# A two-layer sliding-window attention and token-mixing kernel: score bursts of four row tiles, PV in 64x32 tiles with a ones column, normalisation through DRAM, and the first token-mixing matmul in parts inside attention

## The chip, the cores and the metric

The kernel runs on one core of a Trainium2 chip. The metric is the device time of one execution in microseconds (us), quoted as the median of several executions. The engines are called PE (TensorE matmuls), PEld (TensorE weight loads, which overlap PE), DVE (VectorE), ACT (ScalarE), POOL (GpSimd) and SP (SyncE, which issues the DMAs here). An execution counts as slow when it is over 1.5% above the fastest one of the same kernel.

## The reference, cut to what matters

The input is 2048 tokens of 512 features. Two blocks alternate, two layers of each: windowed attention with 32 heads of 16 features (window 256), and an MLP that mixes tokens, with a hidden size of 1792.

```python
def _A_ref(x, wqkv, wo):                       # attention
    H = 32; Dh = 16; W = 256
    q, k, v = ...                              # x @ wqkv, split by heads
    scores = einsum("bhqd,bhkd->bhqk", q, k) * (Dh ** -0.5)
    mask = (i - j >= 0) & (i - j < W)
    p = softmax(where(mask, scores, -1e9))
    return einsum("bhqk,bhkd->bhqd", p, v) ... @ wo

def _B_ref(x, w1, b1, w2, b2):                 # MLP over the tokens
    h = _layernorm(x)
    u = gelu(einsum("bsd,sf->bdf", h, w1) + b1)    # sums over ALL 2048 tokens
    y = einsum("bdf,fs->bds", u, w2) + b2
    return y.transpose(0, 2, 1)

x = x + A(layernorm(x)); x = x + B(layernorm(x))   # twice
```

Attention only looks 256 tokens back, so it runs in four chunks of 512 tokens. And `u` sums over all tokens: each token tile's term of u needs the finished attention, the output projection `wo` and two LayerNorms of that tile, but different tiles' terms can be added up at different times.

## The kernel before

Both kernels record their operations as a graph. A greedy list scheduler inside the kernel then fixes, at build time and with estimated costs, the order of every engine and the place of every buffer. On the chip each engine goes through its list strictly in order.

One group of eight heads (`o`, four groups; a row tile `r` of 32 rows holds two heads) of one chunk (`m`) of attention before, shortened, with plain words for some calls:

```python
for k in ...:                                   # five pieces of 512 score columns (four in chunk 0)
    for u0 in range(0, len(lanes), 2):          # two row tiles per burst
        ts = Tile(psum2)                        # two PSUM banks
        def f_sc(...):
            for j, q0, n, c0 in runs:
                for i, r in enumerate(rr):      # rr = two row tiles of 32 rows
                    e.matmul(PS[:, 2*ts.slot+i, c0*64:(c0+n)*64],
                             lhsT=kbd[32*r:32*r+32, ...], rhs=qT[32*r:32*r+32, ...],
                             tile_position=(32*r, 0), ...)
        op("scalar", exp of both banks -> pt)   # 128 x 1024
    op("vector", f_mask, ...)                   # masks multiplied into pt
# values and denominators: two passes over pt, in 128x32 tiles
for dst, den in ((tO, False), (tDen, True)):
    for r in range(4):
        w = onesbd[:] if den else vbd[:, tkk.slot, jj, 4*o+r, :]
        e.matmul(PS[32*r:32*r+32, 4+dst.slot, ...], lhsT=w, rhs=pt[...], tile_position=(0, 32*r), ...)
# normalisation on the core itself
rl = Ln(tDen); rl = Exp(-rl)                    # ACT, 512 columns each
oT = tO * rl                                    # DVE, straight from PSUM
# ... cut ...
def u_phase(w1t):                               # all of u after attention
    for fb ...: for tt ...: for s0 in range(0, NT, 4):
        matmuls(PS[u], lhsT=w1b[...], rhs=xh_sb[:, sc, :])     # 16 token tiles summed in PSUM
    op("scalar", gelu: PSUM -> uT)
```

The softmax here doesn't subtract the row's maximum and nothing guards it: scores larger than these inputs give would overflow.

Of the kernel before, what the change touches and what calls it, by code (L numbers as in the profile page):

```python
# [2 lines left out]

# [3 lines left out]
dt = mybir.dt  # L7
# [3 lines left out]
P = 128  # L11
INF = float("inf")


class Pool:


    def __init__(self, name, n):
        self.name = name
        self.free = {i: [] for i in range(n)}  # L20
        self.classes = {}
# [14 lines left out]
class Op:  # L36
    __slots__ = ("idx", "eng", "fn", "cost", "lat", "prio", "deps", "users", "ndeps", "tiles", "start", "end",
                 "done", "seq", "dma", "extra", "order")


class Graph:


    ENGS = ("tensor", "vector", "scalar", "gpsimd", "sync")
    NDMA = 24
# [9 lines left out]
    def op(self, eng, fn, reads=(), writes=(), cost=100.0, lat=60.0, prio=None, dma=False, after=(), holds=()):  # L55
        o = Op()
        o.idx, o.eng, o.fn, o.cost, o.lat, o.dma = len(self.ops), eng, fn, cost, lat, dma
        o.prio = prio
        o.users, o.extra, o.order = [], [], []
        deps = {}  # L60
        tiles = {}
# [32 lines left out]
    def _alloc_time(self, o):  # L94

        t, want = 0.0, {}
        for tl in o.tiles:
            if tl.slots is None:
                pool = tl.pool
                n = want[id(pool)] = want.get(id(pool), 0) + tl.n  # L100
                q = pool.classes.get(tl.cls)
                if (q and q[0] + n > q[1]) or len(pool.free) < n:
                    return INF
                ts = sorted(max([x.done for x in ops], default=0.0) for ops in pool.free.values())
                t = max(t, ts[n - 1])
        return t

    def _alloc(self, o):
        for tl in o.tiles:
            if tl.slots is None:  # L110
                pool = tl.pool
                order = sorted(pool.free, key=lambda s: (max([x.done for x in pool.free[s]], default=0.0), s))[:tl.n]
                tl.slots = sorted(order)
                for s in tl.slots:
                    last = {}
                    for x in pool.free.pop(s):
                        if x.dma:
                            last[("d", x.idx)] = x
                        elif x.eng not in last or last[x.eng].seq < x.seq:
                            last[x.eng] = x  # L120
                    o.extra.extend(last.values())
                if tl.cls in pool.classes:
                    pool.classes[tl.cls][0] += tl.n
            tl.ops.append(o)
# [9 lines left out]

    def schedule(self):
# [4 lines left out]
        dma_free = 0.0  # L140
        for o in self.ops:
            if o.ndeps == 0:
                ready[o.idx] = 0.0
                cand[o.eng].append(o)
        left = len(self.ops)
        while left:
            best = None
            for e in self.ENGS:
                m = INF
                ests = []  # L150
                for o in cand[e]:
                    t = max(ready[o.idx], free[e])
                    if any(tl.slots is None for tl in o.tiles):
                        t = max(t, self._alloc_time(o))
                    ests.append(t)
                    if t < m:
                        m = t
                if m < INF and (best is None or m < best[0]):
                    pick = None
                    for o, t in zip(cand[e], ests):  # L160
                        if t <= m:
                            pr = (o.prio if o.prio is not None else ready[o.idx], o.idx)
                            if pick is None or pr < pick[0]:
                                pick = (pr, o)
                    best = (m, e, pick[1])
            if best is None:
                raise RuntimeError("scheduler stuck: " + str({e: len(c) for e, c in cand.items()}))
            m, e, o = best
            cand[e].remove(o)
            self._alloc(o)  # L170
            o.start = m
            if o.dma:
                free[e] = m + 600.0
                dma_free = max(dma_free, m + 600.0) + o.cost
                o.end = dma_free
                o.done = dma_free + 1500.0
            else:
                o.end = free[e] = m + o.cost
                o.done = o.end + o.lat
            o.seq = len(self.order[e])  # L180
            self.order[e].append(o)
            self._release(o)
            for u in o.users:
                u.ndeps -= 1
                ready[u.idx] = max(ready.get(u.idx, 0.0), o.done)
                if u.ndeps == 0:
                    cand[u.eng].append(u)
# [3 lines left out]
    def emit(self, block):  # L191

# [5 lines left out]
        allops = sorted(self.ops, key=lambda o: (o.start, o.idx))  # L198
# [13 lines left out]

# [5 lines left out]
        while pending:  # L218
            moved = False
            for e in self.ENGS:  # L220
                while ptr[e] < len(self.order[e]):
                    o = self.order[e][ptr[e]]
                    need = [d for d in {x.idx: x for x in o.deps + o.extra}.values()
                            if not (e == "tensor" and d.eng == "tensor")]
# [41 lines left out]
def mm_cost(n, cols):  # L266
    return n * (cols / 2.4 + 4.0)
# [10 lines left out]
def pool_cost(n, ptrs=0):  # L278
    return 195 + n / 1.4 + 83 * ptrs


def stepped(v, n, step):

    p, l, c = [list(a) for a in v.ap]
    return bass.AP(v.tensor, v.offset, [p, l, [step, n], c])


def attention_plan(first):

# [18 lines left out]
def bass_interleave_layers__sliding_block__mixer_token_mlp__prompt_kernel(  # L308
# [15 lines left out]
    NC = 4  # L324
# [465 lines left out]
```

## Time and profile before

| | before |
|---|---|
| median time | 593.61 us (4 executions, 592.83 to 595.7) |
| profiled execution | span 589.2 us, mean granted TensorE clock 0.967 |
| attention of layer 1 / layer 2 (first to last exponential) | 172.3 / 194.2 us |
| from the last exponential to the last gelu (the tails) | 63.1 / 67.7 us |

These are lines of the profile's page: busy time of each engine with its share of the span, the chain of work that ended last, and groups of instructions (line, engine, operation, tiles, shapes, count, then busy us and mean ns of one, then idle time before them and what ended most of it).

```profile
PE 533.3 (91%) x6171; PEld 240.1 (41%) x6240; DVE 299.5 (51%) x610; ACT 339.1 (58%) x400; POOL 152.8 (26%) x266
...
PE 57%; ACT 20%; DVE 14%; POOL 4%; DMA 3%; issue 2%; DVEq 0%; POOLq 0%
...
L600 ACT ACTIVATE pt<-PS 128x1024 bf16<-128x1024 f32 (+1 forms) x304 | 288.8, 1033 | 88.1 <-PE PS L587 71.4
L587 PE MATMUL PS<-qT,kbd 32*128 32x320 bf16 (+4 forms) x1440 | 120.9, 262 | 12.0 <-ACT pt L600 9.4
...
L648 PE MATMUL PS<-pt,vbd 128*32 128x320 bf16 (+4 forms) x1440 | 86.4, 270 | 7.7 <-DVE pt L621 2.8
...
L648 PE MATMUL PS<-pt,onesbd 128*32 128x320 bf16 (+4 forms) x1440 | 82.7, 267 | 0.0
```

PE is busy 91% of the span and holds 57% of the chain: as a whole the kernel is bound by PE. 2880 matmuls do values and denominators, half of them only for the denominators.

The next view cuts the span into stages. Each line has the stretch and its length, then the busy time (and count) of PE, PEld, DVE, ACT and POOL, then the granted clock, the DMA share and GB/s. The stretches are attention of layer 1, its tail with u, y and QKV of layer 2, attention of layer 2, its tail, and y with the output.

```profile
17.90:190.20 172.30, 155.77 (x2570) 73.17 (x2588) 118.00 (x245) 155.60 (x182) 68.80 (x109) 0.96 0.10 25
190.20:253.30 63.10, 59.91 (x290) 25.71 (x294) 7.73 (x18) 12.08 (x17) 3.04 (x8) 0.98 0.37 101
253.30:278.80 25.50, 24.07 (x166) 11.93 (x170) 18.03 (x37) 1.33 (x2) 10.31 (x22) 1.00 0.55 150
278.80:473.00 194.20, 180.11 (x2624) 80.19 (x2657) 125.57 (x245) 156.71 (x182) 61.45 (x99) 0.96 0.09 26
473.00:540.70 67.70, 65.24 (x313) 28.07 (x318) 7.73 (x18) 12.12 (x17) 3.04 (x8) 0.98 0.29 78
540.70:589.20 48.50, 39.80 (x173) 17.45 (x176) 11.18 (x16) 0.01 (x1) 0.00 (x0) 0.96 0.53 157
```

Average shares hide the stages: in attention ACT and PE are both busy about 90% of layer 1, while in the first tail PE is busy 60 of 63 us and ACT only 12.

Last, a piece of PE's timeline (start, length, line, tiles, shapes, count). One line can hold several matmuls of a burst; the drawn lengths overlap because ends are modelled, so the burst's pitch is read from the starts.

```profile
71.58 0.39 PE L587 MATMUL PS<-qT,kbd 32*128 32x192 bf16 x4
71.90 1.06 PE L499 MATMUL PS<-xhT,wqkv 128*128 128x512 bf16 x4
72.89 0.39 PE L587 MATMUL PS<-qT,kbd 32*128 32x320 bf16 x4
73.22 0.60 PE L499 MATMUL PS<-xhT,wqkv 128*128 128x512 bf16 x2
...
74.07 0.21 PE L648 MATMUL PS<-pt,vbd 128*32 128x64 bf16 x4
...
74.63 0.31 PE L587 MATMUL PS<-qT,kbd 32*128 32x320 bf16 x2
```

From 71.90 to 72.89 four dense matmuls of 512 columns pass, 0.216 us each plus one gap of about 0.11 us. A score burst takes 0.33 us to the next matmul (72.89 to 73.22), plus the gap ahead of it: 0.43 us for only 0.21 us of streaming. That is the waste that the change goes after. The Trainium skill, "TensorEngine Tiling (Array Packing)", section Key Properties, says that changing the tiling mode drains TensorE; the gaps on both sides of the burst shown here fit it.

### The profile page before, as it was taken

The numbers are of one execution on the slowest core, as the hardware profiler recorded it, in microseconds if no ns is written. First come the engines' busy times: TensorE is split into PE (matmuls) and PEld (weight loads), VectorE is DVE, ScalarE is ACT, GpSimd is POOL, SyncE is SP. The second block draws the span as 40 slices with busy tenths as digits, with TensorE's granted clock in tenths as the row PEclk, the third lists the DMA queues.
The fourth block names the chain that finished last, engine by engine and source line by source line (L and its number), as shares of the span: only waits on it lengthen the run. The fifth ranks groups of instructions, "written<-read, shape, count | busy, mean of one in ns | idle before, by whom it ended". The sixth has DMA issues, their size and how long they took to land.

```text
span 589.2 us, 13839 instructions
## 1 busy us (share of the span) xinstructions
PE 533.3 (91%) x6171; PEld 240.1 (41%) x6240; DVE 299.5 (51%) x610; ACT 339.1 (58%) x400; POOL 152.8 (26%) x266
## 2 busy tenths in 40 slices
PE   4879999999988989989999999999998799997897
PEld 1435444444333434444344434434433343443343
DVE  5986665865873400056766466856687341001021
ACT  0678999699898121110998992299869821111000
POOL 3772433444320200015315212621453001000000
PEclk9989999999995999999999999999999589999899
DMA  8920000000000055572020022202000005251663
GB/s 276 225 54 3 3 1 2 3 2 2 1 2 2 1 143 142 143 197 63 2 63 3 2 59 69 63 3 61 5 2 3 1 1 142 71 143 28 186 187 117
DMA packets 68299, 36.55 MB, mean 62 GB/s; under 512 B 4752, under 2 KB 68240, under 8 KB 68240
## 3 DMA queue, kind: packets, MB, share of 16 engines
q1 hardware_dynamic: 68240, 35.66, 21.8%
q8 instruction: 49, 0.80, 0.6%
q14 instruction: 10, 0.08, 0.0%
HBM read 33.56 MB, written 2.10 MB: 61 GB/s over the span
## 4 chain that ended last, share of the span: by engine, by line
PE 57%; ACT 20%; DVE 14%; POOL 4%; DMA 3%; issue 2%; DVEq 0%; POOLq 0%
ACT pt L600 17%; PE PS L722 15%; PE PS L708 15%; PE PS L587 8%; PE PS L499 7%; PE PS L648 6%; DVE stats L438 4%; PE PS L524 4%; DVE x_sb L677 2%; POOL rstd L449 2%; PE PS L674 2%; DVE pt L621 2%; DVE xh_sb L451 2%; ACT rl L661 1%; ACT rl L663 1%
## 5 line engine op out<-in xcount | busy, mean ns | idle before, releaser
L600 ACT ACTIVATE pt<-PS 128x1024 bf16<-128x1024 f32 (+1 forms) x304 | 288.8, 1033 | 88.1 <-PE PS L587 71.4
L587 PE MATMUL PS<-qT,kbd 32*128 32x320 bf16 (+4 forms) x1440 | 120.9, 262 | 12.0 <-ACT pt L600 9.4
L722 PE MATMUL PS<-uT,w2b 128*128 128x512 bf16 x429 | 105.9, 385 | 10.8 <-DMA w2b<-in_B_w_dram 4.8
L708 PE MATMUL PS<-xh_sb,w1b 128*128 128x512 bf16 x436 | 101.0, 383 | 3.0 <-DVE xh_sb L451 1.0
L726 DVE SCALAR_TENSOR_TENSOR x_sb<-PS,b2col,x_sb 128x512 bf16<-128x512 f32 x32 | 22.9, 746 | 141.8 <-PE PS L722 141.8
L648 PE MATMUL PS<-pt,vbd 128*32 128x320 bf16 (+4 forms) x1440 | 86.4, 270 | 7.7 <-DVE pt L621 2.8
L621 DVE TENSOR_TENSOR pt<-pt,ldm 128x1024 bf16<-128x1024 bf16 (+2 forms) x104 | 65.8, 632 | 52.0 <-ACT pt L600 51.7
L648 PE MATMUL PS<-pt,onesbd 128*32 128x320 bf16 (+4 forms) x1440 | 82.7, 267 | 0.0
L587 PEld LDWEIGHTS PS<-qT,kbd 32*128 32x128 bf16 x1440 | 40.5, 94 | 99.6 <-ACT pt L600 58.1
L715 ACT ACTIVATE uT<-PS,b1col 128x512 bf16<-128x512 f32 x28 | 19.2, 687 | 98.2 <-PE PS L708 98.2
L499 PE MATMUL PS<-xhT,wqkv 128*128 128x512 bf16 x227 | 68.5, 393 | 6.1 <-issue 4.4
L447 POOL TENSOR_SCALAR rstd<-agg 128x1 f32<-128x1 f32 x64 | 16.1, 251 | 220.1 <-DVE agg L440 217.6
L708 PEld LDWEIGHTS PS<-xh_sb,w1b 128*128 128x128 bf16 x448 | 43.3, 98 | 56.8 <-issue 3.2
L510 POOL TENSOR_SCALAR kbd<-stg,par 128x512 bf16<-128x512 bf16 x64 | 50.1, 795 | 62.2 <-DVE stg L507 62.0
L722 PEld LDWEIGHTS PS<-uT,w2b 128*128 128x128 bf16 x448 | 39.4, 98 | 63.2 <-issue 9.4
L536 POOL TENSOR_SCALAR vbd<-stg,half 128x512 bf16<-128x512 bf16 x64 | 49.5, 784 | 48.8 <-DVE stg L533 45.4
L648 PEld LDWEIGHTS PS<-pt,vbd 128*32 128x32 bf16 x1440 | 36.6, 98 | 49.6 <-issue 18.6
L619 DVE TENSOR_TENSOR pt<-pt,ldm 128x512 bf16<-128x512 bf16 (+1 forms) x80 | 32.6, 411 | 22.9 <-ACT pt L600 22.2
L438 DVE BATCH_NORM_STATS2 stats<-x_sb 128x6 f32<-128x512 bf16 x64 | 41.8, 680 | 0.6 <-DMA x_sb<-in_A_x_dram 0.3
L648 PEld LDWEIGHTS PS<-pt,onesbd 128*32 128x32 bf16 x1440 | 38.4, 100 | 3.9
L524 PE MATMUL PS<-wqkv,xhT 128*64 128x256 bf16 x512 | 37.7, 278 | 2.1 <-DVE xhT L490 1.0
L451 DVE TENSOR_SCALAR xh_sb<-x_sb,agg,rstd 128x512 bf16<-128x512 bf16 x64 | 29.0, 456 | 17.7 <-POOL rstd L449 17.1
(36 smaller groups left out, 321.3 us busy)
## 6 DMA issues: line engine op xcount, KB each, us to landing
w1b<-in_B_w_dram SPq DMA_DIRECT2D x14, 1024.0 KB, 6.0
w2b<-in_B_w_dram SPq DMA_DIRECT2D x16, 896.0 KB, 5.6
out_dram<-x_sb SPq DMA_DIRECT2D x16, 128.0 KB, 5.0
wqkv<-in_A_wqkv_dram SPq DMA_DIRECT2D x3, 512.0 KB, 7.1
x_sb<-in_A_x_dram SPq DMA_DIRECT2D x3, 512.0 KB, 8.8
x_sb<-in_A_x_dram SPq DMA_DIRECT2D x2, 256.0 KB, 3.2
wo_sb<-in_A_wo_dram SPq DMA_DIRECT2D x1, 512.0 KB, 9.8
bst<-in_B_b_dram SPq DMA_DIRECT2D x1, 3.5 KB, 9.5
```

Source lines behind the costliest of these rows:

```text
L438: op("vector", lambda e: e.bn_stats(stats[:, t, :], x_sb[:, t, :]), reads=[f"x{t}"], writes=[f"st{t}"], cost=dve_cost(512))
L451: op("vector", lambda e: e.tensor_scalar(xh_sb[:, t, :], x_sb[:, t, :], agg[:, t, 0:1], rstd[:, t, :], op0=ALU.subtract, op1=ALU.mult), re ...
L499: mm_group(ft, 4, lambda e, c: e.matmul(PS[:, 4 + ft.slot, :], lhsT=wqkv[:, c, which * 512 + o * P:which * 512 + (o + 1) * P], rhs=xhT[:, ...
L510: op("gpsimd", lambda e, h=h: e.tensor_scalar(kbd[:, tk.slot, o, :, h, :], stg[:, ts.slot, :].rearrange("p (s n) -> p s n", n=64), par[:, ...
L524: last = e.matmul(PS[64 * hf:64 * hf + 64, 4 + ft.slot, sc * 256:(sc + 1) * 256], lhsT=xhT[:, tx.slot, c, tok:tok + 64], rhs=wqkv[:, c, 10 ...
L536: op("gpsimd", lambda e, h=h: e.tensor_scalar(vbd[:, tk.slot, 2 * sp:2 * sp + 2, :, 16 * h:16 * h + 16], stg[:, ts.slot, :].rearrange("p ( ...
L587: last = e.matmul(PS[:, 2 * ts.slot + i, c0 * 64:(c0 + n) * 64], lhsT=kbd[32 * r:32 * r + 32, tkk.slot, o, jj, :, :].rearrange("p h n -> p ...
L600: return e.activation(pt[:, tp.slot, la:lb + 1:lb - la, 0:n], PS[:, 2 * ts.slot:2 * ts.slot + 2, 0:n], ACTF.Exp, scale=SMSCALE)
L621: return e.tensor_tensor(v, v, msk.unsqueeze(1).unsqueeze(1).to_broadcast([P, lanes, n, w]), op=ALU.mult)
L648: last = e.matmul(PS[32 * r:32 * r + 32, 4 + dst.slot, q0 * 64:(q0 + n) * 64], lhsT=w, rhs=pt[:, tp.slot, ln, c0 * 64:(c0 + n) * 64], star ...
L708: last = e.matmul(PS[:, 2 * tu.slot + tt, :], lhsT=w1b[:, tw.slot, sc, tt * P:(tt + 1) * P], rhs=xh_sb[:, sc, :], start=(sc == 0), stop=(s ...
L722: mm_group(ft, NFT, lambda e, fc: e.matmul(PS[:, 4 + ft.slot, :], lhsT=w2b[:, tw.slot, fc, k * P:(k + 1) * P], rhs=uT[:, fc, :], start=(fc ...
```

## The change

The change rewrites most of the kernel. Its parts:

1. Scores of a piece come as one burst of four row tiles into four PSUM banks (two tiles of two banks, one exponential each), instead of two bursts. The same page of the skill, "Gotcha 1: PSUM Pressure", says that row tiles must write to different PSUM banks; both kernels keep to it, with two banks before and four after.
2. PV works in 64x32 tiles, eight side by side. Each head's 16 value columns are followed by ones (two columns, of which one result is used), so that values and denominators come out of one pass, as a single burst for a whole group.
3. Ln, Exp and the multiply are replaced: DVE evicts both PSUM banks as float32, DMAs carry the result through DRAM into the layout of `oT`, DVE takes the reciprocals of the denominators, DMAs spread them, and Pool multiplies. The last group of the last chunk keeps the old way.
4. u is made in three token parts: chunks 0 and 1 and then chunk 2 are queued before the attention of later chunks is over, into a float32 accumulator in SBUF; chunk 3 comes after attention, with the gelu.
5. PSUM is one pool of eight banks with limits: six for scores, two ("small") for PV and all dense work during attention, six ("big") outside it.

```diff
@@ PSUM @@
-        psum2 = Pool("psum2", 2)
-        psum = Pool("psum", 4)
+        psum = Pool("psum", 8, {"sc": 6, "small": 2, "big": 6})
@@ scores: cut @@
-                        for u0 in range(0, len(lanes), 2):
-                            ts = Tile(psum2)
-                                    for i, r in enumerate(rr):
+                    sa, sb_ = Tile(psum, 2, "sc"), Tile(psum, 2, "sc")
+                        for j, q0, nb, c0 in runs:
+                            for r in range(4):
+                                last = e.matmul(PS[:, bank(r), c0 * 64:(c0 + nb) * 64], ...,
+                                    start=True, stop=True, tile_position=(32 * r, 0), skip_group_check=True)
@@ PV: cut @@
-                                for dst, den in ((tO, False), (tDen, True)):
-                                    for r in range(4):
-                                        w = onesbd[:] if den else vbd[:, tkk.slot, jj, 4 * o + r, :]
+                tO = Tile(psum, 2, "small")
+                    for (runs, _, _), tp in zip(plan, tps):
+                        for j, q0, nb, c0 in runs:
+                            for h in range(2):
+                                for r in range(4):
+                                    last = e.matmul(
+                                        PS[32 * r:32 * r + 18, tO.slots[h], q0 * 64:(q0 + nb) * 64],
+                                        lhsT=vt[64 * h:64 * h + 64, tvv.slot, jj, 4 * o + r, :],
+                                        rhs=pt[64 * h:64 * h + 64, tp.slot, r, c0 * 64:(c0 + nb) * 64],
+                                        start=st, stop=True, tile_position=(64 * h, 32 * r), ...)
@@ normalisation: cut @@
-                (Ln and Exp(-x) of PS[tDen] on ACT, multiply with PS[tO] on DVE: as shown in the kernel before)
+                    return e.tensor_copy(cs[:, tc.slot], PS[:, b0:b0 + 2, :])          # DVE, 1024 columns
+                e.dma_start(scr[td.slot], cs[:, tc.slot])                                # 512 KB to DRAM
+                e.dma_start(rr[:, tr.slot, 0, :], cs[16:P:32, tc.slot]...)               # denominators
+                for h in range(2): e.dma_start(md[64*h:64*h+64, tm.slot, 0, :], scr[td.slot]...)
+                e.reciprocal(rr[:, tr.slot, 1, :], rr[:, tr.slot, 0, :])                 # DVE
+                e.dma_start(rscr[te.slot]..., rr[:, tr.slot, 1, :])
+                for h in range(2): e.dma_start(md[64*h:64*h+64, tm.slot, 1, :], rscr[te.slot, :, h, :] broadcast)
+                e.tensor_tensor(oT, md[..., 0, :], md[..., 1, :], op=ALU.mult)           # Pool
@@ the layer: cut @@
-            w1t = [load_w1(fb) for fb in range(NFT // 2)]
-            u_phase(w1t)
+            tos[1] = attention(1, Q, K, V, direct)
+            prepare(3)
+            wo_block(1, tos[1])
+            u_part([0, 1], True, False)
+            tos[2] = attention(2, Q, K, V, direct)
+            wo_block(2, tos[2])
+            u_part([2], False, False)
+            tos[3] = attention(3, Q, K, V, direct)
+            wo_block(3, tos[3], "big")
+            u_part([3], False, True)
```

## The prediction

> **What bounds the kernel now.** By the windows view, layer 1's attention (28-196 us) has ACT busy 148 of 168 us and PE busy 152; layer 2's (284-481) ACT 154 and PE 183 of 197. In the dense stretches ACT is almost idle: u at 196-256, y and QKV at 256-284, u at 481-545, y at 545-589. Layer 1's attention is bound by ACT (the exponentials come every 0.92 us in runs; 152 a layer make 138 us, and the Ln and Exp of the denominators add about 18), with PE close behind; layer 2's by PE; the rest by PE alone. Chain of waits: exponentials 17%, y 15%, u 15%, scores 8%, PV 6%.
>
> **What a burst costs PE.** In the timeline near 71-76 us a score burst of two row tiles takes 0.21 us of streaming plus about 0.11 us of idle before and after it: 0.43 us in all. The Trainium skill, "TensorEngine Tiling (Array Packing)", section Key Properties, says that changing the tiling mode drains TensorE; these gaps fit. A PV burst (values and ones, four column tiles) takes 0.43 us plus about 0.15.
> - Scores: 304 bursts x 0.43 = 130 us become 152 four-row bursts, about 62 us.
> - PV: 152 bursts of both passes, about 85 us, become 32 bursts of five pieces, about 1.07 us plus 0.2 each: about 41 us.
> - Dense work, estimated at 0.216 us for each 512-column matmul (timeline: pairs 0.45 us apart), stays about 315 us.
> PE's need falls from about 530 to about 420 us.
>
> **ACT.** Ln/Exp go except in one group of sixteen: minus 18 us a layer. Floor of attention 140 us.
>
> **Moved.** Three quarters of u (36 us of PE a layer) goes into attention, where PE now has room. After it about 12 us of u remain, plus the last chunk's wo and LayerNorm (about 10).
>
> **Added.** DVE: 42 u evictions a layer at 0.61 us (pitch of PSUM evictions in its timeline), two thirds of them inside attention (17 us); a 1024-column eviction (estimate 1.15 us) in place of the 0.61 us multiply; reciprocals. DVE in layer 1's attention goes from 110 to about 139 us: three engines near 145. Pool loses the V copies (50 us) and gains 30 multiplies. The normalisation is a chain of some 10-12 us, hidden except in the last group, done directly. DMA traffic (1 MB a group, and w1) stays under the 276 GB/s seen at the start.
>
> **What I think eats part of the gain.** Only two PSUM banks serve PV and all dense work during attention. Each PV takes both until one long eviction ends: 3.5-4 us a group without dense matmuls, of which PE fills half, so about 2 us x 32 = 60 us of PE idle.
>
> **Sum.** Start 18; layer 1 attention about 160 (was 173 from the first exponential); tail with u 24; y and QKV 26; layer 2 attention 195 (was 198, now with u inside); tail, u, y and output 76. About 499 us.
>
> Predicted 499 us, 8 in 10 between 465 and 545. Faster by over 2%: 0.94; within 2%: 0.03; slower: 0.03.
>
> **What would show it.** Score pairs merged into bursts near 0.21 us; PV bursts near 1.1 us with eight tiles running together; exponentials still 0.92 us apart; u stretches shrunk from 55-60 to 12-15 us; PE waiting for DVE's evictions of PV; Ln only twice.
>
> **What would make it wrong.** 64x32 tiles not running together (plus 30 us); DMA issues waiting in order on one queue, so that w1 or normalised output hold PE's fixed order (plus 20-50); or bank lockout smaller than feared (minus 30).

## The result, and the profile after

| | before | after |
|---|---|---|
| median time | 593.61 us | 537.82 us (4 executions: 535.03, 537.68, 537.95, 545.92) |
| ratio of the fast executions | | 0.9044, 95% interval 0.9003 to 0.9085 |
| profiled execution | 589.2 us, clock 0.967 | 536.2 us, clock 0.968 |

The execution of 545.92 us was slow (clock 0.956) and is left out of the ratio. A ratio is the mean time of one kernel's fast runs over that of the other's of the same rounds, so it isn't quite the ratio of the medians.

The kernel became 9.6% faster. The prediction was 499 us, its range 465 to 545: the time lies inside the range, 39 us above its middle.

The page after, in the same order of lines as before, with the two new steps of normalisation that use an engine:

```profile
PE 443.4 (83%) x6754; PEld 208.6 (39%) x6816; DVE 375.9 (70%) x726; ACT 307.0 (57%) x340; POOL 135.1 (25%) x205
...
PE 41%; ACT 27%; DVE 21%; issue 3%; POOL 3%; DMA 3%; SPq 0%; POOLq 0%; DVEq 0%
...
L655 ACT ACTIVATE pt<-PS 128x1024 bf16<-128x1024 f32 (+1 forms) x304 | 280.9, 1041 | 104.0 <-PE PS L643 74.5
...
L643 PE MATMUL PS<-qT,kbd 32*128 32x64 bf16 (+4 forms) x1632 | 62.8, 247 | 40.9 <-ACT pt L655 21.7
...
L753 POOL TENSOR_TENSOR oT<-md 128x512 bf16<-128x512 f32 x30 | 41.2, 1375 | 111.0 <-DMA md<-rscr 111.0
...
L688 PE MATMUL PS<-pt,vt 64*18 64x64 bf16 (+4 forms) x3040 | 38.7, 242 | 7.5 <-DVE pt L668 2.3
...
L731 DVE COPY cs<-PS 128x1024 f32<-128x1024 f32 x30 | 36.4, 1217 | 3.0 <-PE PS L688 2.7
```

Scores fell from 120.9 to 62.8 us of PE and PV, which was two groups of 86.4 and 82.7 that overlap in time (about 85 us by their pitch), became one of 38.7. PE lost 90 us of busy time in all. The span lost only 53: PE's busy share fell from 91 to 83%. DVE rose from 299.5 to 375.9.

The stages after, with the same columns and the same marks (first and last exponential, last gelu) as before:

```profile
18.40:187.40 169.00, 129.54 (x2851) 64.43 (x2870) 134.09 (x257) 140.45 (x152) 57.22 (x76) 0.94 0.43 128
187.40:231.30 43.90, 39.72 (x279) 18.00 (x284) 34.54 (x67) 11.65 (x18) 4.78 (x9) 1.00 0.42 116
231.30:251.00 19.70, 19.49 (x111) 9.11 (x112) 11.18 (x24) 1.30 (x2) 4.54 (x11) 1.00 0.38 105
251.00:432.10 181.10, 152.80 (x2972) 72.27 (x2995) 139.47 (x269) 140.34 (x152) 57.12 (x76) 0.98 0.42 128
432.10:485.80 53.70, 46.25 (x299) 20.13 (x302) 35.65 (x65) 11.93 (x18) 4.92 (x9) 0.94 0.34 97
485.80:536.20 50.40, 46.74 (x212) 20.83 (x215) 11.27 (x16) 0.04 (x1) 0.00 (x0) 1.00 0.53 151
```

Set beside the terms of the predicted sum:

| stage, us | predicted | after | difference |
|---|---|---|---|
| start | 18 | 18.4 | 0 |
| attention, layer 1 | 160 | 169.0 | +9 |
| tail with u | 24 | 43.9 | +20 |
| y and QKV | 26 | 19.7 | -6 |
| attention, layer 2 | 195 | 181.1 | -14 |
| tail with u, y and output | 76 | 104.1 | +28 |
| sum | 499 | 536.2 | +37 |

Both tails are much too long, and layer 2's attention is too short. That pattern is what u would leave behind if it had not gone into attention. The next view shows it directly: the stretches again, but only the matmuls of u from parts (columns: PE, PEld, clock, DMA share, GB/s), with attention cut at the point where the first u appears. A layer has 224 weight loads of u; they are counted in the second bracket of each line, because a few matmul records are missing from the trace.

```profile
18.40:143.00 124.60, 0.00 (x0) 0.00 (x0) 0.92 0.37 111
143.00:187.40 44.40, 22.53 (x89) 7.86 (x96) 1.00 0.57 174
187.40:231.30 43.90, 29.23 (x125) 12.18 (x128) 1.00 0.42 116
251.00:399.00 148.00, 0.00 (x0) 0.00 (x0) 1.00 0.39 120
399.00:432.10 33.10, 19.31 (x67) 6.36 (x73) 0.90 0.53 166
432.10:485.80 53.70, 36.34 (x152) 14.84 (x152) 0.94 0.34 97
```

Only 96 of 224 (43%) and 73 of 224 (33%) went into attention, not the predicted three quarters (168). For the first 125 us of one attention and the first 148 us of the other there is none. What is left after attention is 128 and 151 weight loads; at 0.216 us for each 512-column matmul that is 28 and 33 us, where the prediction had 12.

The single costs came out as predicted. In PE's timeline of the after kernel a four-row burst takes 0.33 us to the next dense matmul and a PV of a whole group 1.30 us:

```profile
312.69 0.40 PE L643 MATMUL PS<-qT,kbd 32*128 32x128 bf16 x12
313.02 0.60 PE L825 MATMUL PS<-ub,w2b 128*128 128x512 bf16 x2
...
318.18 1.36 PE L688 MATMUL PS<-pt,vt 64*18 64x128 bf16 x112 [0.36 <-ACT pt L655]
```

Twelve matmuls for four row tiles cost no more than the four for two row tiles did, so the four run together; 112 PV matmuls that would be about 8.6 us one after the other (5 pieces of 512 columns x 4 column tiles x 2 row halves x 0.216 us) pass in 1.30 us, so the eight tiles run together too. Exponentials stay 0.92 us apart. The failure is not in these.

Why u starts so late is shown by the last normalisation of chunk 1 in layer 1, in the timeline of all engines (SPq is the queue that issues DMAs):

```profile
109.22 1.22 DVE L731 COPY cs<-PS 128x1024 f32<-128x1024 f32 x1
110.46 0.33 SPq L733 DMA_DIRECT2D scr<-cs  x1
...
113.36 1.17 SPq L739 DMA_DIRECT2D md<-scr  x2
115.40 0.34 DVE L743 RECIPROCAL rr<-rr 128x32 f32<-128x32 f32 x1
...
118.25 1.17 SPq L749 DMA_DIRECT2D md<-rscr  x2
...
122.97 1.27 POOL L753 TENSOR_TENSOR oT<-md 128x512 bf16<-128x512 f32 x1 [4.16 <-DMA md<-rscr]
...
144.33 1.67 PE L802 MATMUL PS<-xh_sb,w1b 128*128 128x512 bf16 x7 [0.23 <-issue]
```

The last exponential of chunk 1 ended at 105.1 us and the eviction at 110.4; `oT` is complete at 124.2, 13.8 us later. (The median over the groups is 14.1; predicted were 10 to 12.) The `wo` matmuls of the chunk run until 134.9, LayerNorm follows, and the first u of chunks 0 and 1 comes at 144.3. That is 39 of the 82 us between chunk 1's last exponential and the end of attention. In layer 2 the same stations are 335.7, 349.4, 364.0 and 400.5 us (the first weight load of u): 65 of 96 us are gone. There the PV of the last group starts only at 345.9, 10 us after the last exponential, behind QKV matmuls in PE's order. y stands ahead of `wo`, which begins at 371.1, is interrupted by more QKV for 20 us, and ends at 395.3.

The Trainium skill, "DMA: Bandwidth & Descriptors", section "Anatomy of one DMA — SWDGE (gpsimd) path", gives about 2.0 us fixed for one DMA on that path, mostly the receipt of the last write. This kernel issues from SP, another path; the profile's page shows 3.5 us from issue to landing of the 512 KB write to DRAM, 2.6 us of the values' way back and 3.4 us of the reciprocals'. Several such DMAs in a chain, each waiting for the one before, make the 14 us.

How much PE was idle in attention can be estimated: count the weight loads of each kind in the stretch and give each its measured pitch (512-column dense 0.216 us, a score burst 0.435, a PV burst 1.3). Layer 1 then needs 122 of 169 us, so PE lacks 47; layer 2 150 of 181, so it lacks 31. Before, the same sum left 12 and 10. In layer 1, 38 of the 47 us lie before 142 us, where no u was to be had. The prediction allowed 30 a layer, and for another reason.

### The profile page after: what moved, and what is told of

It is laid out like the page before. It is cut to its first block, busy times and chain, and to the rows that moved or that the text cites. A ratio compares the mean times of both kernels' runs of the same rounds, so it can differ in the third digit from the quotient of the medians.

```text
span 536.2 us, 15441 instructions
## 1 busy us (share of the span) xinstructions
PE 443.4 (83%) x6754; PEld 208.6 (39%) x6816; DVE 375.9 (70%) x726; ACT 307.0 (57%) x340; POOL 135.1 (25%) x205
## 3 DMA queue, kind: packets, MB, share of 16 engines
q1 hardware_dynamic: 91368, 68.25, 42.8%
## 4 chain that ended last, share of the span: by engine, by line
PE 41%; ACT 27%; DVE 21%; issue 3%; POOL 3%; DMA 3%; SPq 0%; POOLq 0%; DVEq 0%
ACT pt L655 27%; PE PS L825 13%; PE PS L802 12%; PE PS L564 4%; PE PS L688 4%; PE PS L643 3%; DVE stats L505 3%; DVE cs L731 3%; PE PS L763 2%; DVE x_sb L767 2%; DVE pt L671 2%; DVE pt L668 2%; DVE xh_sb L516 2%; DVE stg L572 1%; PE PS L589 1%
## 5 line engine op out<-in xcount | busy, mean ns | idle before, releaser
L825 PE MATMUL PS<-ub,w2b 128*128 128x512 bf16 x428 | 101.7, 380 | 2.4 <-issue 1.3
L643 PE MATMUL PS<-qT,kbd 32*128 32x64 bf16 (+4 forms) x1632 | 62.8, 247 | 40.9 <-ACT pt L655 21.7
L671 DVE TENSOR_TENSOR pt<-pt,ldm 128x1024 bf16<-128x1024 bf16 (+1 forms) x80 | 57.2, 716 | 25.5 <-ACT pt L655 25.5
L753 POOL TENSOR_TENSOR oT<-md 128x512 bf16<-128x512 f32 x30 | 41.2, 1375 | 111.0 <-DMA md<-rscr 111.0
L825 PEld LDWEIGHTS PS<-ub,w2b 128*128 128x128 bf16 x448 | 40.7, 98 | 50.0 <-issue 5.2
L575 POOL TENSOR_SCALAR kbd<-stg,par 128x512 bf16<-128x512 bf16 x64 | 47.8, 758 | 48.8 <-DVE stg L572 48.6
L814 DVE TENSOR_TENSOR ub<-PS,ub 128x512 f32<-128x512 f32 x56 | 35.9, 684 | 14.8 <-PE PS L802 14.8
L688 PE MATMUL PS<-pt,vt 64*18 64x64 bf16 (+4 forms) x3040 | 38.7, 242 | 7.5 <-DVE pt L668 2.3
L731 DVE COPY cs<-PS 128x1024 f32<-128x1024 f32 x30 | 36.4, 1217 | 3.0 <-PE PS L688 2.7
L763 PE MATMUL PS<-wo_sb,oT 128*128 128x512 bf16 x121 | 34.6, 403 | 4.7 <-DVE oT L719 3.1
L688 PEld LDWEIGHTS PS<-pt,vt 64*18 64x18 bf16 x3040 | 30.3, 84 | 18.4 <-ACT pt L655 5.3
```

The lines of the kernel that those rows point to most:

```text
L575: op("gpsimd", lambda e, h=h: e.tensor_scalar(kbd[:, tk[o].slot, :, h, :], stg[:, ts.slot, :].rearrange("p (s n) -> p s n", n=64), par[:, ...
L643: last = e.matmul(PS[:, bank(r), c0 * 64:(c0 + nb) * 64], lhsT=kbd[32 * r:32 * r + 32, tkk.slot, jj, :, :].rearrange("p h n -> p (h n)"), ...
L671: return e.tensor_tensor(v, v, msk.unsqueeze(1).unsqueeze(1).to_broadcast([P, 4, k, w]), op=ALU.mult)
L688: last = e.matmul(PS[32 * r:32 * r + 18, tO.slots[h], q0 * 64:(q0 + nb) * 64], lhsT=vt[64 * h:64 * h + 64, tvv.slot, jj, 4 * o + r, :], rh ...
L731: return e.tensor_copy(cs[:, tc.slot], PS[:, b0:b0 + 2, :])
L763: mm_group(ft, 4, lambda e, o, i=i, ft=ft: e.matmul(PS[:, ft.slot, :], lhsT=oT[:, tos[o][0].slot, i * P:(i + 1) * P], rhs=wo_sb[:, 4 if to ...
```

## The experiments

Each variant is the after kernel with one edit. "Change" in the tables is against the after kernel's median of 537.82 us; the kernel before, timed in every set on the same chip, stayed at 592.97 to 593.71 us, so sets compare. Except for the two "thin" kernels the edit makes the scheduler find a new order for every engine. No run changed the order and nothing else, so how much comes from that alone was not measured. The granted clock differs between the runs as well. Three theories were tested: u isn't **ready** in time; the two PSUM **banks** that PV shares with dense work lock PE out (the prediction's fear); **DVE** is overloaded and delays all.

| run | time, us | change | ratio to before [95%] | result | u loads in attention, of 224 |
|---|---|---|---|---|---|
| free_u | 514.43 | -23 | 0.8672 [0.8634, 0.871] | see below | 149, 80 |
| no_norm | 506.57 | -31 | 0.8553 [0.8511, 0.8595] | wrong | 112, 57 |
| banks_4_4 | 526.97 | -11 | 0.8894 [0.8855, 0.8933] | correct | 112, 80 |
| no_masks | 513.47 | -24 | 0.8656 [0.8619, 0.8694] | wrong | 112, 68 |
| short_norm | 527.08 | -11 | 0.889 [0.8862, 0.8918] | wrong | 112, 80 |
| u_last | 569.88 | +32 | 0.962 [0.9584, 0.9657] | correct | 0, 0 |
| pv_two_pass | 546.47 | +9 | 0.9228 [0.919, 0.9265] | correct | 140, 128 |
| banks_wo3 | 510.05 | -28 | 0.8616 [0.858, 0.8651] | correct | 112, 98 |
| thin_masks | 533.71 | -4 | 0.895 [0.889, 0.9011] | wrong | 96, 73 |
| thin_evict | 535.47 | -2 | 0.9015 [0.8974, 0.9055] | wrong | 96, 73 |
| score_pairs | 571.29 | +33 | 0.9602 [0.9559, 0.9644] | correct | 168, 168 |
| banks_wo3_cal | 509.92 | -28 | 0.8577 [0.854, 0.8615] | correct | 112, 93 |

### free_u: u that is ready from the start

The parts of u inside attention take `wqkv` in place of the normalised tokens as input, so they depend on nothing that attention makes. The values are wrong; the result still passed the tolerance. So "correct" says nothing here.

```diff
-    rhs=xh_sb[:, 4 * m + s, :],
+    rhs=xh_sb[:, 4 * m + s, :] if last else wqkv[:, s, 0:512],
-    tws + [f"xh{4 * mm + s}" for mm in chunks for s in range(4)]
+    tws + ["w0"]
```

> Wrong result on purpose: the two parts of u that are meant for attention (chunks 0-1 and 2) read a tile that is ready from the start, so they wait for no wo and no LayerNorm; all else is as after the change. Theory READY (u becomes ready too late, because wo of chunk 1 comes late, so PE idles before and u falls into the tail): in layer 1 the weight loads of u before the last exponential rise from 99 of 224 to 140 or more, the tail from the last exponential to the last gelu shrinks from 44 to about 30 us, and the whole falls by 12 to 20 us (about 520). Theory BANKS (two PSUM banks for PV and all dense work hold PE back): u still can't be placed, under 5 us are won. In layer 2, where y and QKV fill PE, both expect little change.

Measured: 514.43 us, 23 less. The matmuls of u in both attentions and both tails (columns as in the view of u above; the cuts are this kernel's own last exponentials and gelus):

```profile
17.30:180.50 163.20, 38.07 (x148) 11.77 (x149) 1.00 0.48 144
180.50:213.80 33.30, 19.16 (x78) 7.72 (x75) 0.90 0.35 100
235.00:414.10 179.10, 19.94 (x79) 6.60 (x80) 0.99 0.43 130
414.10:462.90 48.80, 35.65 (x146) 14.28 (x144) 0.93 0.36 107
```

In layer 1 u went in (149 loads, up from 96, where 140 or more were expected), attention did not get longer (163.2 against 169.0 us) and the tail fell from 43.9 to 33.3. PE's idle time in layer 1 fell from 47 to 26 us. The 53 more loads are 11.4 us at 0.216, and the tail fell by 10.6. So in layer 1 it was readiness that left u to the tail. The 23 us are more than the 12 to 20 that were expected: attention also got 5.8 us shorter, and there the new order and the clock (1.00 in place of 0.94 in that stretch) can't be told apart. In layer 2 almost nothing changed (80 loads, up from 73; tail 48.8): there readiness alone was not the limit. Over the whole its profile has a clock of 0.983 against 0.968.

### no_norm and short_norm: how much of it is the way through DRAM

no_norm replaces eviction, DMAs, reciprocal and multiply by one DVE copy of 512 columns from PSUM to `oT`. short_norm keeps the work of DVE and Pool (eviction of 1024 columns, reciprocal, multiply) and takes away only the DMAs. Both give wrong values.

```diff
 # no_norm: everything from the eviction to Pool's multiply becomes
+    op("vector", lambda e: e.tensor_copy(oT[:, to.slot, :], PS[:, tO.slots[0], :]), reads=[tO], writes=[to])
 # short_norm: all DMAs removed
-    e.reciprocal(rr[:, tr.slot, 1, :], rr[:, tr.slot, 0, :])
+    e.reciprocal(rr[:, tr.slot, 1, :], cs[:, tc.slot, 0, 0:32])
-    e.tensor_tensor(oT[:, to.slot, :], md[:, tm.slot, 0, :], md[:, tm.slot, 1, :], op=ALU.mult)
+    e.tensor_tensor(oT[:, to.slot, :], cs[:, tc.slot, 0, :], cs[:, tc.slot, 1, :], op=ALU.mult)
```

> Wrong result on purpose: the normalisation through DRAM is left out; DVE copies the 512 columns of the first half straight into oT (one copy of about 0.6 us in place of one of 1.2 us and a reciprocal of 0.3 us), with no DMA and no Pool multiply. Theory NORM (the round trip through DRAM, about 11 us a group, makes wo and then u late): first u in layer 1 moves from about 140 us to 125 or earlier, 12 to 20 us won in all. Theory DVE: about 0.9 us a group come off DVE, 5 to 10 us won. Theory BANKS: the lockout after PV is halved, about 10 us won. READY without NORM: within 5 us.

> Wrong result on purpose: as after the change, with DVE's long eviction, DVE's reciprocal (now of other numbers) and Pool's multiply kept, but no DMA between them: Pool multiplies the two halves of the evicted tile. It parts the two readings of the run without normalisation (31 us won). If the latency and the queueing of the DMA chain (median 14 us from eviction to oT) made wo and u late: about 510 us, and u's first matmul in layer 1 near 125. If it was DVE's extra 1 us a group: about 535, no gain beyond 1%.

Measured: no_norm 506.57 us, 31 less; short_norm 527.08 us, 11 less. In no_norm the first u moved forward from 144.3 to 122.8 us in layer 1 and layer 1's attention fell from 169.0 to 153.2; the last tail fell to 46.7. Taking only the DMAs away brought about a third of that (attention 166.1, tail 45.2 and 46.9). Neither expectation for short_norm came true (510 us, or 535 without a gain), and its first u came at 132.9 us, not near 125. So taking out the DMAs is worth about 11 us, together with what the new order did; the other two thirds go with the work of DVE and Pool, the shorter hold on PV's banks and the new order, which these two runs cannot part.

### banks_4_4: more banks for PV and dense work

```diff
-        psum = Pool("psum", 8, {"sc": 6, "small": 2, "big": 6})
+        psum = Pool("psum", 8, {"sc": 4, "small": 4, "big": 6})
```

> Right result. The class limits of the PSUM pool go from 6 score banks and 2 for PV and dense work to 4 and 4 (the order of all engines is made anew from that). Theory BANKS: PE's idle in the two attention stretches (47 and 31 us) falls by 15 to 25 us and so does the time (about 515). Theories READY and DVE: within 1% of 538, or slower because scores lose their second buffer.

Measured: 526.97 us, 11 less, with a correct result. That lies between the two expectations. PE's idle time, by the same estimate, fell by about 14 us (47 and 31 to 41 and 23), just short of the 15 to 25 of the theory BANKS. The 60 us of lockout that the prediction feared aren't there to be won. The after kernel's waits agree: in both attentions together PE waits only 8.3 us (6.3 + 2.0) for score matmuls that the eviction of PV released. The gain is in layer 2's attention (173.6 us against 181.1); layer 1's attention and both tails moved by less than 2 us (170.1, 42.8 and 52.0).

### no_masks and thin_masks: is DVE too busy

no_masks leaves the masks out, which takes 87 us of DVE's 376 (289 remain) and makes a new order. thin_masks applies each mask to one of four lanes only: the same instructions in the same order of every engine, only shorter, with DVE at 334 us. Both give wrong values.

```diff
 # no_masks
-                    for kind, cells in masks:
+                    for kind, cells in ():
 # thin_masks
-                            v = pt[:, tp.slot, :, cells[0] * 64:cells[0] * 64 + w]
+                            v = pt[:, tp.slot, 0:1, cells[0] * 64:cells[0] * 64 + w]
```

> Wrong result on purpose: the causal and window masks are left out, which takes about 160 us of DVE's 376 busy us away and one dependent step between exponential and PV. Theory DVE (DVE, 80% busy in attention, is what the evictions wait for): 25 us or more won (about 510). Theory BANKS: about 10 us won, since PV's banks are evicted sooner. READY: under 5 us, as the order wo(1) -> u stays.

> Wrong result on purpose, and the order of every engine exactly as after the change: each mask multiply works on one of the four row tiles instead of four (0.74 us becomes about 0.3, 0.43 about 0.2), which takes about 60 us off DVE and holds no PSUM bank. Earlier runs made all orders anew, so they mix the suspected cost with another schedule; this one does not. If DVE's load is what attention waits for: 15 us or more won. If not: under 5 us, and the 24 us of the run without masks came from its other order.

Measured: no_masks 513.47 us, 24 less; thin_masks 533.71 us. thin_masks, fast runs only: 0.895 against 0.9044 for the after kernel, 1% apart, intervals overlapping; its profile, slow, is used only for its busy time. With the order kept, 42 us less DVE work (60 were expected) bought 4 us by the medians and 5 by the fast runs alone. With a new order, 87 us less (160 were expected) bought 24. So DVE's load isn't what this order waits for step by step. That it limits which orders are possible is not shown.

DVE is full at the start of layer 1. Between 40 and 60 us it is busy 20.0 of 20 us in the after kernel (LayerNorms, masks and PSUM evictions). ACT, busy 10.1 us of them, waits 8.9 us (from 33.9 to 42.8) and 6.7 us (until 56.7) for a burst that stands behind a PV in PE's order. In no_masks DVE is busy 12.2 of those 20 us, ACT 19.1, and layer 1's attention takes 153.8 us. But a full DVE does not by itself hold ACT up. In banks_4_4 and banks_wo3 DVE is busy 19.9 and 20.0 of the same 20 us, and ACT 16.7 and 16.5. In banks_4_4 the exponentials of chunk 0 end at 54.4 us in place of 64.2, and yet attention ends at 187.3 us, as in the after kernel (187.4).

### thin_evict: how long PV's banks are held

The eviction of PV copies 64 of 512 columns in each bank, in the same order of every engine (DVE 353.5 us).

```diff
-                    return e.tensor_copy(cs[:, tc.slot], PS[:, b0:b0 + 2, :])
+                    return e.tensor_copy(cs[:, tc.slot, :, 0:64], PS[:, b0:b0 + 2, 0:64])
```

> Wrong result on purpose, order of every engine as after the change (one memset more on Pool at the start): DVE evicts 64 of the 512 columns of each PV bank, 1.2 us becomes about 0.25, 30 times. That takes about 29 us off DVE, half of what the thin masks take, but frees both PV banks a microsecond sooner. If the hold on the two banks costs: more won than with thin masks, 10 to 20 us. If only DVE's load counts: about half of the thin masks' gain. If neither: under 3 us.

Measured: 535.47 us, within the noise of the after kernel (0.9015 against 0.9044). The long eviction, the core of the feared lockout, is not what the given order waits for.

### u_last: none of u in attention

```diff
-            u_part([0, 1], True, False)
             tos[2] = attention(2, Q, K, V, direct)
             wo_block(2, tos[2])
-            u_part([2], False, False)
             tos[3] = attention(3, Q, K, V, direct)
             wo_block(3, tos[3], "big")
-            u_part([3], False, True)
+            u_part([0, 1, 2, 3], True, True)         # gelu straight from PSUM, no accumulator
 # cut: eight w1 buffers in place of four, a smaller ub, the body of u_part
```

> Right result. One part of the change undone: u is computed whole after attention, as before, with gelu straight from PSUM, no accumulator in SBUF and no extra evictions on DVE. If moving u into attention were worth what the prediction said (36 us of PE a layer off the dense stretch, for nothing): 72 us slower than 538. With the measured share of u inside attention (96 and 73 of 224 weight loads) only 21 + 16 us can be lost: 560 to 575. If the extra evictions on DVE had cost attention as much as they saved: no slower than 545.

Measured: 569.88 us, 32 more, inside the 560 to 575 that was expected. The after kernel has 96 + 73 = 169 loads of u in attention, which are 36.5 us of PE at 0.216. Without them in attention the tails grew by 22.9 and 14.6 us, and attention hardly got shorter (167.0 and 174.7 us against 169.0 and 181.1). So most of each us of u that gets in is a us off the tail, and it is too little of it that got in. The granted clock of this run is lower (0.925 against 0.968), so part of the 32 us is PE's clock and not its work. In the tails (clock 0.94 and 0.92, against 1.00 and 0.94) that part is at most about 7 us; in attention it can't be read off.

### pv_two_pass: the old PV and normalisation in the new program

Every group takes the path that the after kernel has for its last group: two passes in 128x32 tiles, Ln, Exp and multiply.

```diff
-        direct = lambda m, o: m == NC - 1 and o == 3
+        direct = lambda m, o: True
+        vbd = sb("vbd", [P, NVU, 4, 16, 32])      # filled by Pool for all V; wo loaded in natural order
 # cut: six q buffers in place of seven, five of oT in place of seven
```

> Right result. One part undone: PV in two passes of 128x32 tiles (values and ones), normalised by Ln and Exp on ACT and a multiply on DVE for every group, no DMA normalisation, V copies on Pool as before; score bursts of four rows and u in parts stay. PE needs about 32 us more and ACT about 36 us more. If PE's and ACT's work rule: 560 or slower. If the late normalisation costs as much as the run without it says (about 30 us): 530 to 550, no loss against 538.

Measured: 546.47 us, 9 more. PV costs more PE time here, attention gets longer (181.1 and 206.6 us against 169.0 and 181.1), but `oT` is ready soon after the last PV, 140 and 128 loads of u go in, and the tails fall to 32.4 and 36.7 us. Parts 2 and 3 of the change together, which the prediction put at 44 us of PE (85 to 41), are worth 9 us of time. At an equal clock they are worth up to some 10 us more: one minus the clock, times the span, is 7 us here (0.987) and 17 us after (0.968). Much of what the cheap PV saves on PE is given back. That the later normalisation is the way, because less of u gets in, fits the counts of loads, but is not shown by itself.

### score_pairs: the old score bursts in the new program

Two bursts of two row tiles each, each with its own two banks (limits 4 and 2 banks). The scheduler's waiting windows are cut as well, from 250 and 150 to 60 ns.

```diff
-                    sa, sb_ = Tile(psum, 2, "sc"), Tile(psum, 2, "sc")
+                    for u in range(2):
+                        ts = Tile(psum, 2, "sc")
-                            for r in range(4):
+                                for r in (2 * u, 2 * u + 1):
 # cut: limits {"sc": 4, "small": 2, "big": 6}, WINDOW = {0: 60.0, 1: 60.0}
```

> Right result. One part undone: score bursts of two row tiles (304 instead of 152), with two pairs of score banks as before the change (class limits 4 and 2) and the scheduler's waiting windows cut to 60 ns, without which it makes a much worse order. PE needs 152 x 0.43 = 65 us more by the pitch in the trace. If PE is what bounds attention: 580 to 610 us. If ACT does: below 560.

Measured: 571.29 us, 33 more, between what the two theories expected (one of its four runs was slow, 581.27 us, and is not in the ratio). The expected 65 us of PE were not there. PE's busy time for scores is 97.3 us, only 34.5 more than the 62.8 of the after kernel, and the time grew by about that (with a clock of 0.936 against 0.968). In the order that the scheduler made, many pair bursts stand next to each other, without the gaps of a change of mode between them, and some of these pairs run together, as one burst of four row tiles would:

```profile
L643 PE MATMUL PS<-qT,kbd 32*128 32x64 bf16 (+4 forms) x1632 | 97.3, 252 | 34.4 <-ACT pt L655 18.5
...
112.92 0.41 PE L643 MATMUL PS<-qT,kbd 32*128 32x128 bf16 x12
113.26 1.94 PE L589 MATMUL PS<-wqkv,xhT 128*64 128x256 bf16 x32
```

These twelve matmuls belong to two pair bursts, and the next matmul starts 0.34 us after them; a single pair burst took 0.33 (110.72 to 111.05). So this run undoes the merging only in part.

Attention grew by 27 and 38 us (196.0 and 219.2), but 168 and 168 loads of u went in, the three quarters that the prediction had counted on, and both tails fell to 28.6 us. The first u came at 138.8 and 409.0 us, not far from the 144.3 and 400.5 of the after kernel, but 78 and 81 us of attention were still to come, in place of 43 and 32. A slower attention gives u time to get ready.

### banks_wo3 and banks_wo3_cal: a better version

banks_wo3 has limits of four banks for scores and three for the rest, and puts the last chunk's `wo` ahead of the waiting u. That came from the end of layer 2 in the after kernel, where PE waits 5.1 us for the last LayerNorm (`xh_sb`) ahead of the last part of u. banks_wo3_cal has four and four banks, and costs in the scheduler nearer to the measured ones.

```diff
-        psum = Pool("psum", 8, {"sc": 6, "small": 2, "big": 6})
+        psum = Pool("psum", 8, {"sc": 4, "small": 3, "big": 6})
+            WPRIO[0] = -1e7                      # wo of chunk 3 before what is left of u
             wo_block(3, tos[3], "big")
+            WPRIO[0] = None
 # banks_wo3_cal besides: small 4, SWITCH 95 -> 110, score cost +14 -> +100, DMA done +1700 -> +2300
```

> Right result; meant as the better version. PSUM class limits 4 for scores and 3 for PV and dense work, and the last wo block of each layer is put ahead of the rest of u in the order of PE, so that its LayerNorm runs beside u. If BANKS and the wait for LayerNorm at the end (5 us in layer 2) add up: the tails from last exponential to last gelu fall from 44 and 54 to about 38 and 45 us, and the whole is 510 to 518. If not additive: near 527, as with the limits of 4 and 4.

> Right result; a second try at the better version: limits 4 and 4, the last wo block first, and the scheduler told the durations that the trace shows (a score burst 0.1 us longer, mode change 0.11 us, DMA 0.6 us later). If the drift between planned and real order costs: 500 to 508. If it is only another order of the same quality: 505 to 515, as banks_wo3.

Measured: 510.05 us and 509.92 us, both correct, 28 less than the after kernel and 14% less than the kernel before. Both expectations were met (510 to 518, and 505 to 515). The two can't be told apart. In banks_wo3 the windows of layer 2's attention and its tail (columns as in the stages) are

```profile
241.00:414.90 173.90, 159.20 (x3025) 73.66 (x3026) 144.33 (x270) 142.47 (x152) 56.69 (x76) 1.00 0.47 142
414.90:455.00 40.10, 37.50 (x273) 17.01 (x271) 33.08 (x61) 11.96 (x18) 5.12 (x9) 1.00 0.34 96
```

Attention fell from 181.1 to 173.9 and the tail from 53.7 to 40.1 us, with PE busy 159 of 174 us and idle in the estimate above only 18.5 us (31 in the after kernel). The first u comes at 127.9 and 376.0 us, not 144.3 and 400.5, and the clock of its profile is 0.990. No gain from the costs in the scheduler can be seen, but banks_wo3_cal has other bank limits too, so they were not tested alone.

## Why the prediction was right and where it was off

The direction and the range were right: faster by over 2% was given 0.94, and 537.82 us is in 465 to 545, though only 7 us below its upper end. Point by point:

1. **"Scores: 304 bursts x 0.43 = 130 us become 152 four-row bursts, about 62 us."** Right: PE's busy time for scores fell from 120.9 to 62.8 us. Burst and gap are 0.33 + 0.11 us, as estimated.
2. **PV "about 41 us".** Right: 30 bursts of 1.30 us (estimated 1.27) and two direct groups of about 2.2 us make 43. The eight 64x32 tiles run together.
3. **"PE's need falls from about 530 to about 420 us."** Right: the sum of weight loads and pitches gives about 422, and PE's busy time fell from 533 to 443.
4. **ACT "minus 18 us a layer".** Nearly right: 15.1 us less in layer 1's attention (155.6 to 140.5) and 16.4 in layer 2's.
5. **DVE "from 110 to about 139 us" in layer 1's attention.** Right in size after (134.1); the start was 118. That DVE is full from 40 to 60 us, with ACT busy for half of it, was not foreseen. Whether this makes the +9 of the first attention is open: no_masks, which clears that stretch, has an attention of 153.8 us in place of 169.0, but banks_4_4 gets through it 10 us earlier and still takes 170.1.
6. **The step that failed: "Three quarters of u (36 us of PE a layer) goes into attention, where PE now has room. After it about 12 us of u remain".** Not 168 but 96 and 73 of 224 loads went in, and 28 and 33 us of u remained: 16 and 21 us more than predicted. Room for PE was there (47 and 31 us of idle time), but in the wrong place. It lay ahead of the point at which chunk 1's normalisation, `wo` and LayerNorm were done, 39 us into the 82 us left in layer 1 and 65 us into the 96 left in layer 2. (In layer 2, 24 of the 28 us that the trace shows as not busy lie before 399 us.) free_u, which takes that dependency away, gets 149 loads in in layer 1 and 23 us off in all, but only 80 loads in layer 2, so the cause is shown for layer 1 and stays open for layer 2; u_last shows that what goes in comes off the tail nearly in full. The term "three quarters" was taken from how u is cut in the source (chunks 0 to 2 of 4), not from when those chunks are ready.
7. **"A chain of some 10-12 us, hidden except in the last group".** The length was nearly right (14.1 us), "hidden" was not: chunk 1's last group is on the way to u as well. short_norm gained 11 us without the DMAs, in another order.
8. **Bank lockout: "about 2 us x 32 = 60 us of PE idle".** Wrong in cause. PE was idle in attention by 78 us, more than feared, but thin_evict, which shortens the hold, changes nothing, banks_4_4 gives 11 us, and PE's waits on the evictions of PV are 8.3 us. The size of the total was near by chance. In layer 1 most of the idle time lay before u was ready (38 of 47 us), which the sum had not foreseen.
9. **Layer 2's attention, 195 predicted, 181.1 measured.** It has 95 fewer loads of u than was assumed (168 - 73), which are 20.5 us at 0.216, and about 4.6 us of dense work more, which the stage before it handed on (PE busy 19.5 us there, 24.1 before the change). Together that is -16, near the -14; it is a sum from the traces, not an experiment. The same loads lengthen the last stage, which also holds the 5.1 us wait for the last LayerNorm that banks_wo3 avoids.

Of the predicted signs in the profile, merged bursts, PV near 1.1 us (1.30), exponentials 0.92 us apart and Ln only twice came true; "u stretches shrunk from 55-60 to 12-15 us" is the one that did not, and the wait for PV's evictions is there but small.

What stays open. no_norm gains 31 us and no_masks 24, and neither is explained by one cause: each changes load, readiness and order at once, and the same-order runs show that load alone is worth 2 to 5 us. What a new order does by itself was not measured in any run. How much of the gain of banks_wo3 is the banks, the early `wo`, or the luck of a new order isn't settled either; banks_4_4 alone gives 11 of the 28 us. In layer 2 free_u gets hardly more u in, and what holds it there was not tested by itself; y and QKV standing ahead in PE's order is argued from the trace, not shown.

## What to carry to other kernels

Work moved into a stage "where the engine has room" pays only from the moment its inputs exist: before counting it, take the end of its last dependency in the trace (here eviction, a chain of DMAs, `wo` and LayerNorm) and count only the room after it. When a change makes the receiving stage faster and its dependencies slower, it shrinks that room from both sides: 43 and 32 us after the first u in the after kernel, 78 and 81 in score_pairs. To tell load from order in a kernel with a fixed schedule, shorten instructions with the order kept (it cost nothing here) before believing what a run with a new order gains. And count the busy time in the trace before taking the number of bursts in the source for the cost: in score_pairs bursts that came to stand side by side cost half of what their number said.

## What the Trainium skill lacked or had wrong

- "TensorEngine Tiling (Array Packing)", section Key Properties: it says that switching the tiling mode drains TensorE, and gives no size. Here it is about 0.11 us on each side of a score burst, half of the 0.43 us that a burst of 512 columns costs, and the reason why merging bursts pays.
- "TensorEngine Tiling (Array Packing)": it lists 64x32 as a mode of eight tiles and gives no time for it; "TensorE: Matmul & The Clock Gate" has times for other tile sizes only. Here the eight run together: 112 matmuls of a whole PV group in 1.30 us.
- "TensorE: Matmul & The Clock Gate", section "Why this matters for your kernels": it asks for "No PE-idle gaps >~3µs between matmul bursts". Here shorter gaps went with a lower granted clock. The same page, section "A second HAM failure mode: psum-queue depth-cycling", does describe short, frequent idle times with a clock that goes up and down, but it gives no size for them. Between 119 and 124.5 us of the after kernel PE's waits were 1.13, 0.51, 1.43 and 0.71 us, and the clock (the third number from the end) fell from 1.00 to 0.50, in these windows of 2 us:

```profile
120.00:122.00 2.00, 0.80 (x24) 0.32 (x24) 1.13 (x2) 2.00 (x3) 0.00 (x0) 1.00 0.72 239
124.00:126.00 2.00, 1.47 (x4) 0.72 (x6) 1.45 (x3) 2.00 (x4) 0.24 (x1) 0.50 0.15 32
```

  Dense matmuls then came 0.43 us apart in place of 0.216. PE was busy 0.80 of 2 us in the first of these windows. So several gaps of 0.5 to 1.4 us close together seem to be enough; which rule the clock follows, no run here shows. The sum of idle time does not decide it: score_pairs had a clock of 0.936 and the after kernel 0.968, with PE not busy for 37 and 29 us of the two attentions against 39 and 28.
- "DMA: Bandwidth & Descriptors": its fit of about 2.0 us plus bytes over the bandwidth is for the gpsimd path; for SP the page has only a first-byte latency (about 600 ns) and no fit for the whole. From SP, a 512 KB write to DRAM took 3.5 us from issue to landing, close to the fit; the 128 KB readbacks took 2.6 us (values) and 3.4 us (broadcast reciprocals), where the fit gives 2.3. A chain of such steps with an eviction and a multiply at its ends took 14.1 us in the median.
